# Four weight pieces on ScalarE's queue, and one 512 KB piece of V on the lower 64 partitions in 8-row transfers

## The chip, the cores and the metric

The kernel runs on one core of one Trainium2 chip. The time is the device time of one execution in microseconds (us), the median of several runs. Engines are written as in the profile: PE (TensorE matmul), PEld (its weight loads), DVE (VectorE), ACT (ScalarE), POOL (GpSimd), SP (SyncE, which issues most of the transfers). The core has 16 DMA engines, which move all transfers whatever engine issued them. A transfer adds 16 in all to its semaphore when it has landed.

## The reference, cut to what matters

Eight sequences (batches) of one token each pass twice through a layer of attention over a cache (A) and a mixing MLP (B). Both layers use the same caches and weights.

```python
B, Sq, D = 8, 1, 448
Hq, Hkv, Sk, Dh = 16, 8, 4096, 256

def _A_ref(x, k_cache, v_cache, wq, wo):
    q = (x @ wq).reshape(B, Sq, Hq, Dh).transpose(0, 2, 1, 3)
    k = jnp.repeat(k_cache, rep, axis=1)
    v = jnp.repeat(v_cache, rep, axis=1)
    p = _softmax(jnp.einsum("bhqd,bhkd->bhqk", q, k) * (Dh ** -0.5))
    o = jnp.einsum("bhqk,bhkd->bhqd", p, v)
    return o.transpose(0, 2, 1, 3).reshape(B, Sq, Hq * Dh) @ wo

x = x + _A_ref(_layernorm(x), k_cache, v_cache, wq, wo)
x = x + _B_ref(_layernorm(x), w1, w2, w3, w4)
x = x + _A_ref(_layernorm(x), k_cache, v_cache, wq, wo)
x = x + _B_ref(_layernorm(x), w1, w2, w3, w4)
```

With a sequence of one token the mixing of layer B adds nothing, so w1 and w2 aren't read: B is a norm, w3, gelu and w4. All numbers are bf16. One head of one batch has 4096 x 256 of K and as many of V, 2 MB each; there are 64 of each.

## The kernel before

**Tiles.** K and V live in a slab of 31 slots of 512 KB (128 partitions of 4 KB; `SLOT`, `NSLOT`, line 387). A head of K or V is four pieces ("chunks") of 512 KB, `c` = 0 to 3; partition p holds rows 32 p to 32 p + 31 of the cache, and piece c eight of these. Two heads `s` = 0, 1 are a pair, `m` = 0 to 3, of batch `b`. `chunks` (line 452) makes the load units of one head: `most` neighbouring pieces go in one transfer (512 KB, 1 MB or 2 MB), to as many neighbouring slots.

**Stages.** `kpart` computes the scores of a pair and their softmax: K is transposed on DVE (line 938) or on PE (line 856), multiplied with q on PE, and the exponentials P are written to `pT` (three buffers) with a transposed order of rows; some are also kept apart in `pN` (two buffers). `vpart` multiplies P with V on PE: with P as the moving side and V's 128x128 blocks as weights for the pairs called still (line 1089), with P as weights and V moving otherwise (line 1115); in the second form it then gathers the four partial sums (lines 1126 to 1141). `outproj8` applies wo (line 1178). `turn` is the MLP of one batch between its two attention layers, `end` the MLP of all batches at the very end. K of pairs 1 to 3 stays in its slots from the first layer to the second.

**Order.** Nothing of the order is written by hand: `Plan.schedule` simulates all engines with a cost for each operation and lays out the sequence of each engine's instructions. Among operations that are ready it takes the one with the smallest `prio`. Transfers go in the order of the list `order` (line 1278); each waits until its slots are free in that simulation, and each counts as 330 ns of SP. Groups of four or two can be split when no run of slots is free (lines 268 to 277). Every engine then runs its sequence in order, and waits on semaphores at what the plan found to be dependences.

**The start.** wq and w3 have 448 rows: three blocks of 128 and a rest of 64, which is folded into 128 partitions as two pieces of 64 partitions, `wqt0`, `wqt1` (256 KB each) and `w3t0`, `w3t1` (112 KB each). Piece 0 lies on partitions 0 to 63, piece 1 on 64 to 127. The pieces 1 (`U_side`) are issued from ACT's queue at the very start (line 1364); the pieces 0 (`U_even`) by SP, ahead of x (`U_s0`, 8 rows) and of the first K.

**The end.** In the last batch (b = 7) of the second layer, V comes in the order pair 1, 2, 3, 0 (lines 1267 and 1274), pair 3 in transfers of four pieces, pair 0 in transfers of two. Pair 0 is the last and is still: each piece is 16 matmuls of line 1089.

Of the kernel before, what the change touches and what calls it, by code (L numbers as in the profile page):

```python
# [3 lines left out]
P = 128  # L4
B = 8
# [6 lines left out]
NCH = 4  # L12
NSLOT = 31
SMALL = 220
SLOT = 2048
AHEAD = (1, 2)
NT = 2
NS = 2
NV = 2
# [54 lines left out]
class Unit:  # L74


    def __init__(self, name, emit, nbytes, slotted=True):
        self.name, self.emit, self.nbytes, self.slotted = name, emit, nbytes, slotted
        self.wide = None
        self.slot = self.sem = self.val = None  # L80
        self.op = None
        self.readers = []
        self.land = None
        self.evs = [None, None]
        self.raw, self.source = False, None
        self.side = False
        self.group, self.lead, self.pair = [self], None, None


class Plan:  # L90
# [79 lines left out]
    def schedule(self, order, nslot):  # L170
# [77 lines left out]
        while remaining or nxt[0] < len(order):  # L248
# [8 lines left out]
            while nxt[0] < len(order):  # L257
                u = order[nxt[0]]
                if any(d.end is None for d in u.op.deps):
                    break  # L260
                start = max(free["sp"], max((d.end + 80 for d in u.op.deps), default=0.0))
                us = u.group
                if u.slotted:
                    if len(us) == 1:
                        best = single(t)
                    else:
                        best, short = run(t, len(us))
                        if short and len(us) == 4 and transfer < t + DRY4:
# [12 lines left out]
                    start = max([start] + [slot_free[best + k][0] for k in range(len(us))])  # L281
                if start > t + 1e-6:
                    sp_next = start
                    break
                if u.slotted:
                    for k, x in enumerate(us):
                        _, waits = slot_free.pop(best + k)
                        x.slot = best + k
                        for w in waits:
                            u.op.deps[w] = True  # L290
                        live.append(x)
                        if x.raw:
                            raw.add(x)
                free["sp"] = start + 330.0
                if u.emit is not None:
                    transfer = max(start + 3300.0, transfer) + (P * 4096 * len(us) / 415.0 if len(us) > 1 else u.nbytes / 410.0)
                    land = transfer + 2000.0
                else:
                    land = start
                for x in us:  # L300
                    x.land = land
                u.op.on = "sp"
                seq["sp"].append(u.op)
                done(u.op, land, 0.0)
                nxt[0] += 1
                progress = True
# [54 lines left out]
def bass_interleave_layers__gqa_block_cached__mixer_s_mlp__decode_kernel(  # L361
# [33 lines left out]
    ident = sb("ident", [P, P], bf)  # L395
# [36 lines left out]
    def rows(u, t, ap, nbytes):  # L432
# [3 lines left out]
    U_wq = [rows(f"wq{k}", wq_sb[:, k, :], A_wq[k * P:(k + 1) * P, :], P * 8192) for k in range(3)]  # L436
    U_wq += [rows(f"wqt{i}", wqt_sb[64 * i:64 * i + 64, :], A_wq[3 * P:D, 2048 * i:2048 * i + 2048], 64 * 4096)
             for i in range(2)]
    U_side = [U_wq.pop()]
    U_w3 = [rows(f"w3{k}", w3_sb[:, k, :], B_w3[k * P:(k + 1) * P, :], P * 3584) for k in range(3)]  # L440
    U_w3 += [rows(f"w3t{i}", w3t_sb[64 * i:64 * i + 64, :], B_w3[3 * P:D, 896 * i:896 * i + 896], 64 * 1792)
             for i in range(2)]
    U_side.append(U_w3.pop())
    for u in U_side:
        u.side = True
    U_even = [U_wq.pop(), U_w3.pop()]
    wq_rest, w3_rest = ([U_side[i], U_even[i]] for i in range(2))
# [4 lines left out]
    def chunks(cache, b, h, name, skip=(), most=2):  # L452


        src = cache[b, h].rearrange("(p j) d -> p (j d)", p=P)

        def emit(e, u):
            c, n = int(u.name[-1]), len(u.group)
            return e.dma_start(slab[:, SLOT * u.slot:SLOT * (u.slot + n)], src[:, SLOT * c:SLOT * (c + n)])
        us = [None if c in skip else Unit(f"{name}{c}", emit, P * 4096) for c in range(NCH)]  # L460
        for i in range(0, NCH, most):
            group = [u for u in us[i:i + most] if u is not None]
            if len(group) == most:
                plan.load(group[0], mates=group[1:])
            else:
                for u in group:
                    plan.load(u)
        return us


    Bc = Buf()
# [388 lines left out]
    def kpart(at, layer, b, m, kept, most=2):  # L860
# [13 lines left out]
        p.x = x  # L874
        p.y = y = free_p.pop(0)
        p.z = z = free_n.pop(0) if layer == 0 and m > 1 else None
        plan.prio = at
        p.K, p.kload = [], []
        for s in range(2):
# [166 lines left out]
            430, [], [BpT[y]], [bS[x]], prio=pr, name=n + "pq")  # L1046
        for o in plain:
            plan.ops[-1].deps[o] = o.eng == "dve"
        for c in range(nn if z is None else 0):
            ss = slice(sum(c >= w for w in nns), 2)  # L1050
            add("act", lambda e, c=c, ss=ss: e.activation(apart(pT[y])[:, :, c, :, ss], xs.rearrange("p (a c r s) -> p a c r s", a=4, c=4, r=4)[:, :, c, :, ss],
# [6 lines left out]
    def vpart(at, p, still, bank, most, aside):  # L1058
# [5 lines left out]
        p.V = [u for s in range(2) for u in chunks(A_v_cache, b, 2 * m + s, f"{n}V{s}", (), most)]  # L1064
        p.vload = [u for u in p.V if u.lead is None]
        if layer == 0:
            out_, bo = o1[b % 2][:, 8 * m:8 * m + 8], Bo1[b % 2][m]
        else:
# [30 lines left out]
        else:  # L1099
# [3 lines left out]
            for s in range(2):  # L1103
                for c in range(NCH):
                    u = p.V[NCH * s + c]

                    def pv(e, u=u, c=c, s=s):
# [10 lines left out]
                    o = add("pe", pv, 430, Bp(s, c), [], [bV[x]], [u], prio=at + 0.02 * (NCH * s + c), name=f"{n}V{s}{c}", n=4)  # L1118
                    if s or c:
                        o.deps[first] = True  # L1120
                    else:
# [28 lines left out]
        if z is not None:  # L1150
            free_n.append(z)

    Bst = [{k: Buf() for k in ("pm", "gm", "mx")} for _ in range(NS)]

# [120 lines left out]
                weave(V(1, b, m, most=4 if m else 2))  # L1275
    plan.prio = 1e9
    U_out = end()
    order = U_side[:1] + U_even[:1] + U_side[1:] + U_even[1:] + [U_s0] + stream[:1] + U_wq + stream[1:10] + U_wo + stream[10:]
    order.append(U_s1)
    order.append(U_out)  # L1280
    seq = plan.schedule(order, NSLOT)
# [143 lines left out]
```

## Time and profile before

| what | value |
|---|---|
| runs | 1095.83, 1095.85, 1096.48 us; median 1095.85 |
| the profiled execution | 1096.3 us, of which the span of instructions is 1094.5 |
| busy, share of the span | PE 70%, PEld 48%, DVE 76%, ACT 19%, POOL 7% |
| transfers | 448.96 MB, mean 410 GB/s; 427 GB/s from 1036 to 1056 us |
| the chain that ended last | DVE 39%, DMA 26%, PE 20%, issue 7%, ACT 3% |
| granted PE clock, mean | 0.616 |
| SP's longest waits in total | for PE's V products of line 1115 294 us, for PE's scores of line 947 217 us |

A row of the stretches view has, after the stretch and its length, the busy time of PE, PEld, DVE, ACT and POOL with the number of their instructions, the granted PE clock, the DMA share (mean busy share of the 16 engines; packets that overlap on an engine can take it over 1) and GB/s. A row of the time order has start, duration, engine, line, operation, output and inputs, count, and in brackets the idle time before it and what ended it. A row of transfers has output and input, the issuing queue, count, KB of one and the median us from issue to landing.

The start, as the time order has it: ACT issues `wqt1` at 0.73 and `w3t1` at 1.32 us; SP issues `wqt0` at 0.74 (0.58 us), `w3t0` at 1.37 (0.83), x at 2.25 (0.53), the first K at 2.83 (0.37), then wq and more K. `ident`, which the first transposes need, is written by POOL at 9.94 us. The last three transfers of V are issued from 1051.88 to 1052.84 us.

### The profile page before, as it was taken

What the parts mean: (1) busy time and instruction counts of PE and PEld (TensorE: products, weight loads), DVE (VectorE), ACT (ScalarE), POOL (GpSimd) and SP (SyncE); (2) the same over time, 40 slices, a digit from 0 to 9 for tenths busy, and PEclk for the clock granted to TensorE, in tenths of its full rate; (3) what the DMA queues carried; (4) which work ended last, traced back from release to release, by engine and by line L of the source; (5) the groups of instructions that cost most, each with busy time, mean ns of one, the idle gap of its engine ahead of it and who ended that gap; (6) DMA issues with size and microseconds to landing.
All of it is one profiled execution on the core that took longest, in us unless ns stands there. A gap on an engine that the chain in (4) does not pass through costs nothing.

```text
span 1094.5 us, 33709 instructions
## 1 busy us (share of the span) xinstructions
PE 764.3 (70%) x15416; PEld 525.1 (48%) x15416; DVE 830.5 (76%) x1567; ACT 212.2 (19%) x322; POOL 72.0 (7%) x232
## 2 busy tenths in 40 slices
PE   3467586778677865778667786578766795676865
PEld 3255453465346543565336654365433654346533
DVE  5899549964997499954999569974799839996572
ACT  1023131113011311203202032121221231111310
POOL 0000000000000000000000010000100000000000
PEclk9998566556655665556655566555565666655655
DMA  9999999999999999999999999999999999999994
GB/s 357 405 420 417 411 400 428 422 404 409 428 422 417 411 428 426 422 395 423 426 426 419 399 423 426 426 416 398 427 428 424 400 406 426 426 423 414 416 425 188
DMA packets 54703, 448.96 MB, mean 410 GB/s; under 512 B 5520, under 2 KB 11552, under 8 KB 14112
## 3 DMA queue, kind: packets, MB, share of 16 engines
q1 hardware_dynamic: 54400, 446.42, 98.3%
q8 instruction: 121, 1.98, 0.7%
q10 hardware_dynamic: 160, 0.38, 0.1%
q14 instruction: 22, 0.18, 0.0%
HBM read 446.77 MB, written 0.01 MB: 408 GB/s over the span
## 4 chain that ended last, share of the span: by engine, by line
DVE 39%; DMA 26%; PE 20%; issue 7%; ACT 3%; POOL 1%; SPq 0%; DVEq 0%; POOLq 0%
DVE slots L938 31%; DMA slots<-in_A_k_cache_dram 17%; DMA slots<-in_A_v_cache_dram 9%; PE psV L1115 5%; PE psS L947 4%; DVE pT L1045 2%; PE psS L926 2%; PE psV L1089 2%; PE psT L609 1%; ACT slots L916 1%; DVE slots L1128 1%; PE psT L695 1%; PE psT L1163 1%; PE psK L856 1%; ACT slots L1217 1%
## 5 line engine op out<-in xcount | busy, mean ns | idle before, releaser
L938 DVE STREAM_TRANSPOSE slots<-slots 128x1024 bf16<-128x1024 bf16 x544 | 647.7, 1230 | 38.2 <-DMA slots<-in_A_k_cache_dram 25.1
L947 PE MATMUL psS<-qe,slots 128*128 128x8 bf16 x5760 | 225.4, 174 | 165.2 <-DVE slots L938 107.5
L947 PEld LDWEIGHTS psS<-qe,slots 128*128 128x128 bf16 x5760 | 190.5, 103 | 250.1 <-DVE slots L938 173.0
L1115 PE MATMUL psV<-slots,pT 128*8 128x512 bf16 x1528 | 183.7, 555 | 20.0 <-DMA slots<-in_A_v_cache_dram 15.2
L916 ACT COPY slots<-psK 128x1024 bf16<-128x1024 bf16 x80 | 78.6, 1015 | 165.1 <-PE psK L856 164.6
L856 PE MATMUL psK<-ident,slots 128*128 128x128 bf16 x640 | 75.1, 304 | 3.1 <-DMA slots<-in_A_k_cache_dram 2.9
L1009 POOL PARTITION_ALL_REDUCE small<-small x64 | 23.9, 374 | 720.4 <-DVE small L1007 586.0
L1126 ACT ACTIVATE slots<-psV 128x512 bf16<-128x512 f32 x48 | 28.8, 600 | 201.9 <-PE psV L1115 201.9
L856 PEld LDWEIGHTS psK<-ident,slots 128*128 128x128 bf16 x640 | 62.4, 141 | 5.7 <-DMA slots<-in_A_k_cache_dram 3.5
L975 PE MATMUL psS<-slots,qe 128*8 128x512 bf16 x200 | 55.3, 593 | 6.5 <-DVE slots L938 6.4
L1089 PE MATMUL psV<-pT,slots 128*128 128x2 bf16 x1568 | 50.6, 165 | 9.6 <-DMA slots<-in_A_v_cache_dram 9.0
L1115 PEld LDWEIGHTS psV<-slots,pT 128*8 128x8 bf16 x1528 | 31.5, 90 | 52.6 <-DMA slots<-in_A_v_cache_dram 21.5
L1089 PEld LDWEIGHTS psV<-pT,slots 128*128 128x128 bf16 x1568 | 47.2, 104 | 11.6 <-DMA slots<-in_A_v_cache_dram 9.1
L1128 DVE TENSOR_TENSOR slots<-psV,slots 128x512 bf16<-128x512 f32 x48 | 32.5, 677 | 25.2 <-ACT slots L1126 25.0
L1030 ACT ACTIVATE pT<-psS 128x128 bf16<-128x128 f32 x56 | 15.6, 279 | 173.6 <-DVE psS L1027 173.4
L1045 DVE STREAM_TRANSPOSE pT<-psS 128x128 bf16<-128x128 bf16 x64 | 45.2, 706 | 4.4 <-PE psS L1037 2.2
L1137 PE MATMUL psV<-same,slots 128*128 128x4 bf16 x320 | 14.2, 166 | 41.9 <-DVE slots L1128 36.8
L1163 PE MATMUL psT<-small,wo_sb 128*128 128x1 bf16 x1024 | 35.7, 166 | 7.1 <-DVE small L1096 4.7
L926 PE MATMUL psS<-qo,slots 128*128 128x2 bf16 x768 | 28.0, 167 | 13.4 <-ACT slots L916 10.4
L1163 PEld LDWEIGHTS psT<-small,wo_sb 128*128 128x128 bf16 x1024 | 32.5, 105 | 9.2 <-DVE small L1096 6.0
L1137 PEld LDWEIGHTS psV<-same,slots 128*128 128x128 bf16 x320 | 11.8, 103 | 49.6 <-issue 42.3
L1096 DVE TENSOR_TENSOR small<-psV,small 128x4 bf16<-128x4 f32 x30 | 4.3, 144 | 41.1 <-PE psV L1089 41.1
(178 smaller groups left out, 768.8 us busy)
## 6 DMA issues: line engine op xcount, KB each, us to landing
slots<-in_A_v_cache_dram SPq DMA_DIRECT2D x149, 1024.0 KB, 9.9
slots<-in_A_v_cache_dram SPq DMA_DIRECT2D x50, 2048.0 KB, 21.1
slots<-in_A_k_cache_dram SPq DMA_DIRECT2D x45, 2048.0 KB, 21.1
slots<-in_A_k_cache_dram SPq DMA_DIRECT2D x69, 1024.0 KB, 14.3
slots<-in_A_v_cache_dram SPq DMA_DIRECT2D x14, 512.0 KB, 8.0
wo_sb<-in_A_wo_dram SPq DMA_DIRECT2D x4, 896.0 KB, 19.1
wq_sb<-in_A_wq_dram SPq DMA_DIRECT2D x3, 1024.0 KB, 11.3
w_sb<-in_B_w_dram SPq DMA_DIRECT2D x1, 1568.0 KB, 15.2
```

Source lines behind the costliest of these rows:

```text
L856: last = e.transpose(tile[:, j * P:(j + 1) * P], slots[u.slot][:, o:o + P], ident[:, :])
L916: return e.copy(slots[u.slot][:, 1024 * t:1024 * t + 1024], tile)
L926: last = e.matmul(o, slots[u.slot][:, i:i + P], q, start=(cc == 0), stop=(cc == 1))
L938: return e.transpose(o, i)
L947: last = e.matmul(o, slots[u.slot][:, i:i + P], qe[:, 128 * k + 64 * s + 8 * g:128 * k + 64 * s + 8 * g + 8], start=(g == 0), stop=(g == 7))
L975: last = e.matmul(o, q, K[:, lo:hi + 1:hi - lo, :, g, :], start=(g == 0), stop=(g == 7))
L1045: add("dve", lambda e: e.transpose(pZ[:, :, 0:3:2].rearrange("p n s r -> p n r s"), psS[x][:, 128:192].bitcast(bf).rearrange("p (n r s) -> ...
L1089: last = e.matmul(o, slots[u.slot][:, i:i + P], w, start=(c == 0 and cc == 0 and j == 0), stop=(c == NCH - 1 and cc == 1 and j == 7))
L1115: last = e.matmul(psV[x][32 * i:32 * i + 8, :].rearrange("p (k d) -> p k d", k=2), w, v, start=(s == 0 and c == 0), stop=(s == 1 and c == ...
L1126: add("act", lambda e: e.activation(part(0), psV[x][:, :], ACT.Copy), 590, [], [Bhalf[0]], [bV[x]], [v], prio=at - 1, name=n + "ve0").targ ...
L1128: add("dve", lambda e: e.tensor_tensor(part(1), psV[x][:, :], part(0), ALU.subtract), 590, [Bhalf[0]], [Bhalf[1]], [bV[x]], [v], prio=at - ...
L1163: last = e.matmul(psT[:, 4 * (2 * s + i) + c:4 * (2 * s + i) + c + 1], wo_sb[:, a, d0:d0 + P], o1[b % 2][:, a:a + 1], start=(k == 0), stop ...
```

## The change

1. All four rest pieces go to ACT's queue, `wqt1`, `wqt0`, `w3t1`, `w3t0`; SP begins with x, then the first K.
2. In batch 7 of the second layer, pair 3, head 0, piece 3 of V (`LOW`): its upper 64 rows no longer go to the upper 64 partitions of a slot but to the lower 64 of a second slot. Each half is eight transfers of 8 rows; transfer i takes the rows r0, r0 + 4, ..., r0 + 28 with r0 = 32 (i // 4) + i % 4, to the partitions of the same numbers. The rest of that head goes as one pair of pieces and one single piece, where it could be one transfer of four.
3. P has to follow: a matmul with the right half of `ident` brings the upper 64 rows of P for that piece to the lower 64 partitions of PSUM, and ACT copies them to a `pN` buffer. The product of that piece is eight matmuls over 64 partitions instead of four over 128.
4. The last head of pair 0 (`B7m0V1`) is loaded in four single pieces instead of two pairs.
5. The plan counts 330 ns of SP for each of a unit's issues, and a slot's semaphore 16 for each.

```diff
+LOWS, LOWC = 0, 3
+def LOW(layer, b, m, s):
+    return (layer, b, m, s) == (1, B - 1, 3, LOWS)
...
-                free["sp"] = start + 330.0
+                free["sp"] = start + 330.0 * u.issues
...
-    U_side = [U_wq.pop()]
+    wq_rest = U_wq[3:]
+    del U_wq[3:]
...
-    U_side.append(U_w3.pop())
+    w3_rest = U_w3[3:]
+    del U_w3[3:]
+
+    U_side = wq_rest[::-1] + w3_rest[::-1]
     for u in U_side:
         u.side = True
-    U_even = [U_wq.pop(), U_w3.pop()]
-    wq_rest, w3_rest = ([U_side[i], U_even[i]] for i in range(2))
...
+        if low:
+            def half(p0):
+                def emit(e, u):
+                    for i in range(8):
+                        r0 = 32 * (i // 4) + i % 4
+                        d = e.dma_start(slots[u.slot][r0:r0 + 29:4, :], src[p0 + r0:p0 + r0 + 29:4, SLOT * LOWC:SLOT * (LOWC + 1)])
+                        if i < 7:
+                            d.then_inc(u.sem, 16)
+                    return d
+                return emit
+            most = 2
+            us[LOWC] = Unit(f"{name}{LOWC}", half(0), 64 * 4096)
+            us[LOWC].upper = Unit(f"{name}u{LOWC}", half(64), 64 * 4096)
+            us[LOWC].issues = us[LOWC].upper.issues = 8
         for i in range(0, NCH, most):
             group = [u for u in us[i:i + most] if u is not None]
-            if len(group) == most:
+            if len(group) == most and not name.startswith(f"B{B - 1}m0V1") and all(u.upper is None for u in group):
                 plan.load(group[0], mates=group[1:])
             else:
                 for u in group:
-                    plan.load(u)
+                    for w in (u, u.upper):
+                        if w is not None:
+                            plan.load(w)
...
+        if p.low:
+            low = psS[x][0:64, 192:208].rearrange("p (a r) -> p a r", a=4)
+            add("pe", lambda e: e.matmul(low, ident[:, 64:P], apart(pT[y])[:, :, p.place(LOWS, LOWC), :, LOWS], start=True, stop=True),
+                110, [BpT[y], Bc], [], [bS[x]], prio=pr, name=n + "lo", n=1)
+            add("act", lambda e: e.copy(apart(pN[zl])[0:64, :, 0, :, LOWS], low), 230, [], [BpN[zl]], [bS[x]], prio=pr, name=n + "lc")
...
+                    def low(e, u=u, c=c, s=s):
+                        for i in range(4):
+                            o, i_ = 12 * (NCH * i + p.place(s, c)) + 4 * s, 12 * i + 4 * s
+                            for w, v in ((pT[y][0:64, o:o + 8], u), (pN[p.zl][0:64, i_:i_ + 8], u.upper)):
+                                last = e.matmul(psV[x][32 * i:32 * i + 8, :].rearrange("p (k d) -> p k d", k=2), w,
+                                                slots[v.slot][0:64].rearrange("p (k j d) -> p j k d", k=2, j=4)[:, i], start=False, stop=False)
+                        return last
...
-    order = U_side[:1] + U_even[:1] + U_side[1:] + U_even[1:] + [U_s0] + stream[:1] + U_wq + stream[1:10] + U_wo + stream[10:]
+    order = [U_s0] + U_side + stream[:1] + U_wq + stream[1:10] + U_wo + stream[10:]
...
-            slot_n[u.slot] += 16
+            slot_n[u.slot] += 16 * u.issues
```

More of the change, by code (lines that the diff above doesn't have):

```diff
@@ L86, in __init__ @@
         self.side = False
+        self.upper = None
+        self.issues = 1
         self.group, self.lead, self.pair = [self], None, None
@@ L450, in bass_interleave_layers__gqa_block_cached__mixer_s_mlp__decode_kernel, with chunks @@
     U_w4 = [rows("w4", w4_sb[:, :, :], B_w4.rearrange("(t m) n -> m t n", m=P), P * 12544 * 1.1)]
-    def chunks(cache, b, h, name, skip=(), most=2):
+    def chunks(cache, b, h, name, skip=(), most=2, low=False):
         src = cache[b, h].rearrange("(p j) d -> p (j d)", p=P)
@@ L876, in kpart @@
         p.z = z = free_n.pop(0) if layer == 0 and m > 1 else None
+        p.low = LOW(layer, b, m, LOWS)
+        p.zl = zl = free_n.pop(0) if p.low else None
         plan.prio = at
@@ L1063, in vpart @@
         plan.prio = at
-        p.V = [u for s in range(2) for u in chunks(A_v_cache, b, 2 * m + s, f"{n}V{s}", (), most)]
-        p.vload = [u for u in p.V if u.lead is None]
+        p.V = [u for s in range(2) for u in chunks(A_v_cache, b, 2 * m + s, f"{n}V{s}", (), most, LOW(layer, b, m, s))]
+        p.vload = [w for u in p.V if u.lead is None for w in (u, u.upper) if w is not None]
         if layer == 0:
@@ L1117, in pv @@
                         return last
-                    o = add("pe", pv, 430, Bp(s, c), [], [bV[x]], [u], prio=at + 0.02 * (NCH * s + c), name=f"{n}V{s}{c}", n=4)
+                    def low(e, u=u, c=c, s=s):
[5 more added lines that the diff above has]
+                        return last
+                    if u.upper is not None:
+                        o = add("pe", low, 860, Bp(s, c) + [BpN[p.zl]], [], [bV[x]], [u, u.upper], prio=at + 0.02 * (NCH * s + c), name=f"{n}V{s}{c}", n=8)
+                    else:
+                        o = add("pe", pv, 430, Bp(s, c), [], [bV[x]], [u], prio=at + 0.02 * (NCH * s + c), name=f"{n}V{s}{c}", n=4)
                     if s or c:
@@ L1149, in vpart @@
         free_p.append(y)
-        if z is not None:
-            free_n.append(z)
+        for z_ in (z, p.zl):
+            if z_ is not None:
+                free_n.append(z_)
     Bst = [{k: Buf() for k in ("pm", "gm", "mx")} for _ in range(NS)]
```

## The prediction

> **What bounds the kernel.** I read the page first: the transfers.
>
> ```profile
> span 1094.5 us, 33709 instructions
> ...
> DMA  9999999999999999999999999999999999999994
> ...
> q1 hardware_dynamic: 54400, 446.42, 98.3%
> q8 instruction: 121, 1.98, 0.7%
> ```
>
> The sixteen DMA engines are busy in every slice but the last, so the time is the bytes over some 424 GB/s, plus a start, plus a tail behind the last landing. DVE (76%) and PE (70%) have room on average. The fetching of instructions (q8) costs 0.7% of 16 x 1094.5 us over 121 fetches: 1.0 us of one engine for each. So I looked where DMA is not full: the start, the end and the turns between batches. The stretches of the start:
>
> ```profile
> 2.00:3.00 1.00, 0.00 (x0) 0.00 (x0) 0.78 (x4) 1.00 (x1) 0.00 (x0) 1.00 0.71 188
> 3.00:4.00 1.00, 0.00 (x0) 0.00 (x0) 0.87 (x3) 0.25 (x1) 0.00 (x0) 1.00 1.04 274
> 4.00:5.00 1.00, 0.00 (x0) 0.00 (x0) 0.09 (x2) 0.00 (x0) 0.00 (x0) 1.00 1.01 215
> 5.00:6.00 1.00, 0.00 (x0) 0.00 (x0) 0.00 (x0) 0.00 (x0) 0.00 (x0) 1.00 1.32 264
> 6.00:7.00 1.00, 0.00 (x0) 0.00 (x0) 0.00 (x0) 0.00 (x0) 0.00 (x0) 1.00 0.73 262
> 7.00:8.00 1.00, 0.00 (x0) 0.00 (x0) 0.00 (x0) 0.00 (x0) 0.00 (x0) 1.00 0.98 410
> ```
>
> The last two columns are DMA share and GB/s. The engines are occupied from 3 us on, but move 215 to 274 GB/s, about half of the 424 seen later, while the four 64-partition pieces (wqt, w3t) are written: half of the partitions take half the rate. From 3 to 8 us 1.43 MB moved where 2.12 could have: 1.6 us lost. The end:
>
> ```profile
> 1076.00:1077.00 1.00, 0.71 (x27) 0.63 (x25) 0.19 (x1) 0.00 (x0) 0.00 (x0) 0.50 0.98 410
> 1077.00:1078.00 1.00, 1.00 (x41) 1.00 (x39) 0.24 (x1) 0.00 (x0) 0.00 (x0) 0.50 0.96 401
> 1078.00:1079.00 1.00, 0.73 (x28) 0.65 (x25) 0.48 (x3) 0.00 (x0) 0.00 (x0) 0.50 0.70 295
> 1079.00:1080.00 1.00, 0.48 (x16) 0.40 (x15) 0.19 (x1) 0.00 (x0) 0.00 (x0) 0.50 0.43 180
> 1080.00:1081.00 1.00, 0.95 (x32) 0.93 (x32) 0.00 (x0) 0.00 (x0) 0.00 (x0) 0.50 0.26 98
> 1081.00:1082.00 1.00, 0.06 (x3) 0.00 (x0) 0.00 (x0) 0.00 (x0) 0.00 (x0) 0.50 0.06 25
> ```
>
> The share runs out over four us: the engines don't finish together. The trace's completion counts (each engine adds one to a transfer's semaphore) give it singly for the last transfer: the first engine at 1078.18 us, the others 0.1, 0.1, 0.5, 0.7, 0.9, 1.3, 1.3, 1.8, 2.5, 2.7, 2.8, 2.8, 2.9, 3.1 and 4.3 us later. The last matmuls wait for that last one:
>
> ```profile
> 1080.05 1.01 PE L1089 MATMUL psV<-pT,slots 128*128 128x2 bf16 x32 [0.56 <-DMA slots<-in_A_v_cache_dram]
> 1082.51 1.01 PE L1089 MATMUL psV<-pT,slots 128*128 128x2 bf16 x32 [1.44 <-DMA slots<-in_A_v_cache_dram]
> 1083.55 0.18 DVE L1096 TENSOR_TENSOR qo<-psV,small 128x4 bf16<-128x4 f32 x1 [3.77 <-PE psV L1089]
> ```
>
> PE waits for the last megabyte until 1082.51, then needs 1.01 us for its 32 matmuls; the rest is a chain to 1094.5. Whatever brings the last landing forward shortens the kernel by as much.
>
> **Which engines are late.** Following the counts from transfer to transfer, each fetch of instructions puts one engine back by about 1.5 us, in turn over the same eight engines; the other eight are hit by the rare q14 fetches alone. The x transfer has 8 rows, and its count arrives as one jump and eight single steps: eight engines carry it. Six of these eight are among the late ones at the first K transfer, where five of the six late ones belong to those that fetches never hit. So I hold the eight engines of an 8-row transfer to be the unburdened ones; this is inferred, not shown.
>
> The Trainium skill ("DMA: Bandwidth & Descriptors", Why a DMA increments its semaphore by 16 and not by 1) says that the transfer runs on as many engines as divide its outer size, up to 16, and on this queue on the lowest-numbered ones. The x count of nine steps agrees with eight; which eight, no row shows.
>
> **Part 1, the start.** SP loses two issues (0.58 and 0.83 us) ahead of x and the first K; ScalarE's queue gains two of about 0.6 us, so its table load at 1.96 us ends 1.2 us later, 9 us before ACT's first work at 13.55. The DMA engines were already occupied without a gap from 2.07 us, so an earlier issue adds no bytes; the same pieces still go to the same halves at half rate, only with K between them. Nor does an earlier landing of x or K0 help: ident, which both wait for, comes from POOL at 10.2 us, and the norm's root waits for POOL until 19.86. Value 0; bounds -1.6 us (all of the lost rate comes back) and +0.3 (upper and lower pieces overlapped a little before, the row 274, and no longer do). A side effect: with x first, the list scheduler can put the root's DVE operations ahead of the first square (13.61, 1.23 us), which would then run after 21 us. DVE's next room covers that:
>
> ```profile
> 50.00:60.00 10.00, 3.90 (x68) 2.74 (x65) 6.46 (x7) 0.97 (x2) 0.37 (x1) 1.00 1.01 423
> ```
>
> 3.5 us of DVE are free there; without them it is +1.2.
>
> **Part 2, the pieces of the last batch.** One engine takes 159, 309 or 611 ns for a row of 4, 8 or 16 KB (medians of the packet records) and 9 ns for a completion. Head 0 of pair 3 was one transfer with 8 rows of 16 KB an engine: 4.89 us. Now a pair (8 x 0.309 = 2.47), a single (8 x 0.159 = 1.27), and sixteen 8-row transfers of one row an engine: 16 x 0.159 + 15 x 0.009 = 2.68 on eight engines, nothing on the other eight. The eight take 6.42 (+1.5), the others 3.74 (-1.15). The last head of pair 0 in four singles instead of two pairs: 32 x 0.159 + 4 x 0.009 against 16 x 0.309 + 2 x 0.009, +0.16 for all. Together +1.7 and -1.0. If the burdened eight are the eight latest, the last of them ends at 4.3 - 1.0 = 3.3 and the last of the others at 1.3 + 1.7 = 3.0: -1.0. If the one at 1.8 or 2.5 is of the others (a q14 fetch hit one at 1002 us), that one ends at 3.5 to 4.2: -0.8 to -0.1. I take -0.6; bounds -1.0 and +1.7 (the last engine itself is one of the eight that take more).
>
> **Part 3, the tail.** The last landing holds one piece instead of two; the piece before it lands some 1.2 us earlier and is done meanwhile. 16 matmuls instead of 32: -0.5. Bounds -0.5 and 0.
>
> **Part 4, costs I put at nothing.** SP: 17 more issues for pair 3 and 2 for pair 0, 19 x 0.377 us (median of the nine there) = 7.2 us, 10.1 at the x issue's 0.53. Behind them wait pair 3's second head and all of pair 0. Cover: in this stretch transfers land long after issue,
>
> ```profile
> slots<-in_A_v_cache_dram SPq DMA_DIRECT2D x5, 2048.0 KB, 19.9
> slots<-in_A_v_cache_dram SPq DMA_DIRECT2D x4, 1024.0 KB, 26.7
> ```
>
> for 5 and 2.5 us of moving, so over 14 us of queue stand ahead. Without that cover, +7 to +10. PE: four matmuls more (four took 0.39 us at 1066.5) and one of 16 columns, in a stretch where it waits 3.6 us for DMA; ACT's copy of 0.3 us falls in an idle time of 3.2 us; the slot more is taken when K slots have been given back (last K scores at 1061). Their P is ready 10 us before use. If the cover went, 0.3 to 0.7 us.
>
> **Sum.** 0 - 0.6 - 0.5 = -1.1 us on the profiled execution, 1096.3 us (1094.5 of span and 1.8 around it), which lies 0.45 over the median 1095.85: the median becomes 1094.8.
>
> **Rivals.**
> A, the start pays: K between the half pieces lets their writes catch up and 1.6 us comes back, which the unbroken DMA carries to the end; with half of the spread of part 2: 1095.85 - 1.1 - 1.6 - 0.2 = 1092.9. For: 215 GB/s is waste. Against: the bytes per half are unchanged.
> B, small transfers pay a fixed price on the eight engines, at pair 3's last piece. From 3.0 + 16p > 3.3, p = 0.02 us, they end last; at p = 0.11 the gain is gone; at 0.25 it is 0.2% slower. Nearest row: the 1.6 us lost between 3 and 8 us over five small transfers, 0.32 each: 16 x 0.32 = 5.1, the end at 8.1 instead of 4.3, less 0.5: +3.3, 1099.2. Against: the stretch 1036 to 1056 has a share of 100% with transfers back to back. The Trainium skill ("DMA: Bandwidth & Descriptors", Rules for kernel authors) says that transfers under 64 KB are mostly overhead and should be joined; by its 0.68 us for 4 KB the sixteen would be an estimated 11 us. The start's rows lie below that.
> C, the plan is made anew: the earlier x shifts choices of the list scheduler, and other slots come free late at the turns, where the queue nearly drains (361 GB/s at 140 to 150 us). One square (1.23 us) late in four of eight turns: +4.9 - 1.1, 1099.7. Against: the transfers' order and lengths are the same until the last batch.
> D, the 8 rows use all engines, or the wrong eight: only the tail is left, 1095.4.
>
> **How the numbers follow.** Forecast 0.50, A 0.17, B 0.15, C 0.13, D 0.05. Its own range is 1093.4 to 1096.1. The joint one, 1092.5 to 1098.6, takes in most of A, D, and B and C where they are mild. 0.2% (2.2 us) is about what a measurement here tells from no change: faster A and an edge of the forecast, 0.22; slower most of B and C, 0.26; same 0.52.
>
> **What would show it.** Right: the DMA share at the end falls within some three us instead of four, the last PE group has 16 matmuls, the start still shows 215 to 270 GB/s and wq lands as before. Wrong: over 400 GB/s by 5 us (A); the end held up by eight engines alone, a share of 0.5 for long (B); other turns, lower GB/s there (C).

## The result and the profile after

| | before | after |
|---|---|---|
| runs, one next to the other | 1094.05 to 1098.37 us, median 1095.61 (13) | 1095.63 to 1100.08 us, median 1097.36 (13) |
| the profiled execution | 1096.3 us, span 1094.5 | 1099.78 us, span 1098.0 |
| the last landing of V | 1082.46 us | 1086.41 us |
| from there to the end of the span | 12.04 us | 11.59 us |

The ratio is 1.0021, with a 95% interval of 1.0012 to 1.0030: the change makes the kernel slower, by 1.3 to 3.3 us. The profiled execution of after is 2.4 us over its own median, so its span of 1098.0 isn't to be set against 1094.5 as a whole; what follows compares stretches. The page of after:

```profile
DMA  9999999999999999999999999999999999999994
...
q1 hardware_dynamic: 54928, 446.04, 98.2%
```

As before, DMA is full in all slices but the last. The packets of q1 (SP's queue) are 528 more: the smaller pieces of V add more than the two rest pieces take away that went to ACT's queue. The fetches of instructions are 121, as before. The stretches of the start of after (DMA share and GB/s last):

```profile
5.00:6.00 1.00, 0.00 (x0) 0.00 (x0) 0.00 (x0) 0.00 (x0) 0.00 (x0) 1.00 1.02 422
6.00:7.00 1.00, 0.00 (x0) 0.00 (x0) 0.00 (x0) 0.00 (x0) 0.00 (x0) 1.00 1.14 303
7.00:8.00 1.00, 0.00 (x0) 0.00 (x0) 0.00 (x0) 0.00 (x0) 0.00 (x0) 1.00 0.96 233
8.00:9.00 1.00, 0.00 (x0) 0.00 (x0) 0.00 (x0) 0.00 (x0) 0.00 (x0) 1.00 0.97 276
9.00:10.00 1.00, 0.00 (x0) 0.00 (x0) 0.00 (x0) 0.00 (x0) 0.00 (x0) 1.00 1.05 369
10.00:11.00 1.00, 0.00 (x0) 0.00 (x0) 0.00 (x0) 0.00 (x0) 0.00 (x0) 1.00 1.00 342
11.00:12.00 1.00, 0.03 (x1) 0.04 (x2) 0.06 (x1) 0.00 (x0) 0.28 (x1) 1.00 1.04 337
12.00:13.00 1.00, 0.23 (x4) 0.14 (x4) 0.73 (x10) 0.00 (x0) 0.00 (x0) 1.00 0.98 332
```

The slow stretch that ended at 7 us before now lasts to 13 us, at a full DMA share. Before, the stretches from 7 to 13 us moved 410 to 442 GB/s. K comes through from 5 to 6 us, but the rest pieces then trickle: the completion counts show `wqt0` landed at 9.86, `w3t1` at 12.10 and `w3t0` at 13.82 us, where before all four had landed by 6.72. The packet records show the delay in the rows of K and wq too: one of 8 KB takes a median of 473 ns from 6 to 9 us and 378 ns from 9 to 13 us, and 309 ns in before from 100 us to 1000 us. Adding the GB/s column from 2 to 13 us gives 3.73 MB before and 3.40 MB after: 0.33 MB less, or 0.8 us at 424 GB/s. The end of after, in stretches:

```profile
1081.00:1082.00 1.00, 1.00 (x41) 1.00 (x39) 0.36 (x1) 0.00 (x0) 0.00 (x0) 0.50 0.86 340
1082.00:1083.00 1.00, 0.77 (x29) 0.69 (x27) 0.37 (x2) 0.00 (x0) 0.00 (x0) 0.50 0.52 213
1083.00:1084.00 1.00, 0.78 (x29) 0.70 (x27) 0.16 (x1) 0.00 (x0) 0.00 (x0) 0.50 0.19 78
1084.00:1085.00 1.00, 0.54 (x16) 0.46 (x16) 0.04 (x1) 0.00 (x0) 0.00 (x0) 0.50 0.17 70
1085.00:1086.00 1.00, 0.58 (x16) 0.50 (x16) 0.00 (x0) 0.00 (x0) 0.00 (x0) 0.50 0.08 29
1086.00:1087.00 1.00, 0.54 (x16) 0.50 (x16) 0.00 (x0) 0.00 (x0) 0.00 (x0) 0.50 0.06 16
```

and PE in order of time:

```profile
1083.96 0.58 PE L1123 MATMUL psV<-pT,slots 128*128 128x2 bf16 x16 [0.22 <-DMA slots<-in_A_v_cache_dram]
1085.20 0.58 PE L1123 MATMUL psV<-pT,slots 128*128 128x2 bf16 x16 [0.66 <-DMA slots<-in_A_v_cache_dram]
1086.46 0.58 PE L1123 MATMUL psV<-pT,slots 128*128 128x2 bf16 x16 [0.67 <-DMA slots<-in_A_v_cache_dram]
```

From 1083 us on the share is 0.19 and less: some three of sixteen engines still work, and then one, and PE takes one piece of 16 matmuls after the other as these engines bring them. The counts of the last transfer lie 0, 0.7, 1.5, 1.5, 1.6, 2.1, 2.2, 2.2, 2.5, 2.5, 2.7, 2.9, 3.0, 4.5, 4.9 and 5.8 us after the first: a spread of 5.8 us, where before it was 4.3. What follows the last landing is 0.45 us shorter.

### The profile page after: what moved, and what is told of

Read it like the earlier page. It is cut to its first block, busy times and chain, and to the rows that moved or that the text cites. A ratio compares the mean times of both kernels' runs of the same rounds, so it can differ in the third digit from the quotient of the medians.

```text
span 1098.0 us, 33739 instructions
## 1 busy us (share of the span) xinstructions
PE 762.1 (69%) x15421; PEld 523.7 (48%) x15421; DVE 830.8 (76%) x1567; ACT 212.4 (19%) x323; POOL 71.6 (7%) x232
## 4 chain that ended last, share of the span: by engine, by line
DVE 36%; DMA 27%; PE 21%; issue 8%; SPq 4%; ACT 4%; POOL 1%; DVEq 0%; POOLq 0%
DVE slots L966 27%; DMA slots<-in_A_k_cache_dram 15%; DMA slots<-in_A_v_cache_dram 12%; PE psV L1149 6%; PE psS L975 5%; SPq L440 3%; DVE pT L1073 2%; PE psS L954 2%; PE psV L1123 2%; DVE slots L1173 1%; PE psT L635 1%; ACT slots L944 1%; SPq L469 1%; PE psK L882 1%; ACT slots L1263 1%
```

## The experiments

Three numbers are read from each profile besides the time. **L12**: the mean landing (over the sixteen counts) of the thirteenth transfer to the slots, a transfer of K issued at 45.4 to 47.4 us, which shows how far the start is behind; the expectations call it the thirteenth K transfer. **Spread**: from the first to the last count of the last transfer of V. **To end**: from the mean landing of the last transfer of pair 1 of batch 7 to the end of the span (which is read to 0.1 us); it leaves out all that happened before. Diffs are against the changed kernel where nothing else is said. "The start of before" is

```diff
-    wq_rest = U_wq[3:]
-    del U_wq[3:]
+    U_side = [U_wq.pop()]
...
+    U_even = [U_wq.pop(), U_w3.pop()]
+    wq_rest, w3_rest = ([U_side[i], U_even[i]] for i in range(2))
...
-    order = [U_s0] + U_side + stream[:1] + U_wq + stream[1:10] + U_wo + stream[10:]
+    order = U_side[:1] + U_even[:1] + U_side[1:] + U_even[1:] + [U_s0] + stream[:1] + U_wq + stream[1:10] + U_wo + stream[10:]
```

and "the end of before" is

```diff
-    return (layer, b, m, s) == (1, B - 1, 3, LOWS)
+    return False
...
-            if len(group) == most and not name.startswith(f"B{B - 1}m0V1") and all(u.upper is None for u in group):
+            if len(group) == most and all(u.upper is None for u in group):
```

All in one table; the text on each follows. The ratios are to runs of the kernel before made next to them (medians 1095.38 to 1095.78 us); they aren't the quotient of two medians, and where the two columns differ the text goes by the ratio and its interval.

| kernel | median, us | ratio, 95% interval | MB, 2 to 13 us | L12, us | spread, us | to end, us |
|---|---|---|---|---|---|---|
| before | | 1 | 3.73 | 56.26 | 4.28 | 44.27 |
| after | 1097.36 | 1.0021 [1.0012, 1.0030] | 3.40 | 57.08 | 5.77 | 44.80 |
| start_only | 1098.13 | 1.0013 [1.0002, 1.0024] | 3.25 | 57.63 | 4.13 | 44.06 |
| start_plan | 1094.76 | 0.9999 [0.9986, 1.0011] | 3.78 | 56.16 | 3.43 | 43.35 |
| start_pairs | 1097.02 | 1.0008 [0.9997, 1.0018] | 3.72 | 56.32 | 3.10 | 43.30 |
| start_sp | 1096.50 | 1.0002 [0.9992, 1.0012] | 3.77 | 56.60 | 4.22 | 44.27 |
| start_mix | 1095.86 | 1.0003 [0.9993, 1.0014] | 3.68 | 56.39 | 2.94 | 43.29 |
| low_only | 1096.99 | 1.0004 [0.9993, 1.0015] | | 55.90 | 5.87 | 44.97 |
| end_only | 1095.58 | 0.9997 [0.9987, 1.0007] | | 56.39 | 6.14 | 44.68 |
| low_twice | 1097.44 | 1.0021 [1.0011, 1.0031] | | 56.38 | 5.59 | 45.72 |
| low_16 | 1098.25 | 1.0017 [1.0008, 1.0027] | | 56.17 | 4.09 | 46.94 |
| singles_only | 1095.00 | 0.9997 [0.9985, 1.0008] | | 56.08 | 4.13 | 44.04 |
| end_plain | 1095.69 | 0.9993 [0.9983, 1.0004] | | 56.21 | 4.00 | 43.59 |
| probe | 1094.14, one run | | | 56.33 | 3.40 | 43.54 |

**The parts alone.** start_only has the end of before, so of the change it keeps the four pieces on ACT's queue and x first.

> Only the start of the change: all four rest pieces on ScalarE's queue, SP begins with x and K; the last batch as before. Theory S (mixing half-partition pieces with K costs DMA time): the K transfers issued in the first 7 us land on the mean of the sixteen engines 0.8 us later than before (first engine +1.0, last engine about 0), from 20 to 120 us, and the kernel takes 0 to +0.8 us. Rival (the start is free, as predicted): mean within 0.2 us, time 0. Rival C (a new plan): other jumps at the turns, present in every run.

The start alone is slower by 0.13% (0.2 to 2.6 us), and L12 is 1.4 us late, more than the 0.8 of after and the 0.8 that was expected. The trace has the same slow stretches, 221 to 344 GB/s from 6 to 13 us. The end is that of before in every number.

low_only has the start of before and pair 0 in pairs; only the piece in 8-row transfers is left:

```diff
-            if len(group) == most and not name.startswith(f"B{B - 1}m0V1") and all(u.upper is None for u in group):
+            if len(group) == most and all(u.upper is None for u in group):
```

> Only the piece in 8-row transfers; the start and the last head of pair 0 (two pairs) as before. Theory L (some of the eight engines that carry the 8-row transfers are among the late ones): the last transfer's sixteen counts spread over 5.5 to 6 us instead of 4.3, its last count is 1.2 to 2.0 us further behind pair 2's last transfer than before, and the kernel takes +1.0 to +2.0 us. As predicted (the eight are the unburdened ones): spread about 3.3, time -0.6. Rival B (a fixed price p for each small transfer): the eight engines are behind by 1.5 + 16 p, all of them alike, so that the last counts of the piece come at more than 0.25 us from one another on each engine.

The spread is 5.9 us, and "to end" is 1.2 us over the mean of the seven kernels that end as before (43.29 to 44.27, mean 43.73), and 0.7 us over before alone. The time, 1.0004, doesn't show it: its interval (0.8 us faster to 1.6 slower) holds both nothing and 1.2 us.

singles_only has the start of before and `LOW` returns False; the last head in four single pieces is left.

> Only the last head of pair 0 in four single pieces; start and pair 3 as before. Theory: 0.16 us more of transfers for rows of 4 KB, and 16 matmuls instead of 32 behind the last landing, -0.45 us from the last landing to the end: 12.04 becomes 11.6; the kernel takes -0.3 us. Rival (the four issues or the smaller rows cost as much as the tail gives): 0.

The part behind the last landing is 11.66 us, 0.4 less than the 11.92 to 12.09 of the kernels with pairs. The time is that of before within its interval. end_plain is the same, and takes the change's division of pair 3's head 0 (a pair and two single pieces) too, but in ordinary transfers over 128 partitions:

```diff
+        if name.startswith(f"B{B - 1}m3V0"):
+            most = 2
...
-            if len(group) == most and not name.startswith(f"B{B - 1}m0V1") and all(u.upper is None for u in group):
+            if len(group) == most and not (name.startswith(f"B{B - 1}m0V1") or name.startswith(f"B{B - 1}m3V0") and i == 2) and all(u.upper is None for u in group):
```

> Pair 3's head 0 as a pair and two single pieces, piece 3 in one ordinary transfer over 128 partitions, the last head of pair 0 in four singles; the start as before. What is left of the end of the change when no small transfers and no uneven load are in it. Theory L: no cost but smaller rows, +0.3 us of transfers, -0.45 of tail: -0.1 us, the last spread 4.3 as before. Rival (the splitting itself, with its issues and slots, is what costs): +1 us or more here too.

Its spread is 4.0 us, so the division of the head doesn't widen it; the 8-row form does. It has the lowest ratio of all, 0.9993, but the interval reaches over 1, so it can't be called faster than before.

**What of the start costs.** start_plan keeps the changed order of all instructions, the DVE operations of the norm's root ahead of the squares included, and issues the transfers as before. The end of before is in all four of these.

```diff
         if e == "act":
-            for u in U_side:
+            for u in U_side[0::2]:
                 u.emit(eng, u).then_inc(u.sem, 16)
+        if e == "sp":
+            for u in U_side[1::2]:
+                u.emit(eng, u).then_inc(u.sem, 16)
```

> The instruction order of the changed kernel at the start (the two squares of DVE behind the root), but the four rest pieces are issued as before: uppers from ACT, lowers by SP ahead of x and K. The end is that of before. Theory S (the time goes where half-partition pieces share the engines with whole transfers): the mean landing of the thirteenth K transfer is at 56.3 us as before, the time within 0.1% of before. Rival D (the squares' late place costs): the landings at 57 us or later, and the time of start_only, +0.13%.

L12 is at 56.16, the ratio 0.9999 (1.5 us faster to 1.2 slower): the order of DVE costs nothing up to L12 and nothing that the time shows, as theory S has it. start_pairs puts x first on SP, then the lower pieces on SP beside the upper ones on ACT (`U_side[0::2]` alone is issued from ACT and marked as side).

> x goes first on SP, and then the rest pieces lower and upper side by side from SP and ACT again, all ahead of the first K. The end is that of before. Theory S: like before, the thirteenth K lands at 56.3 us in the mean, time within 0.1%. Rival X (it is the early x that costs): 57.1 to 57.6 us and +0.13%. If only the last lower piece still overlaps K, between the two, some +0.3 us.

The landings are those of before (56.32), so the early x costs nothing up to there either. The time, 1.0008, lies between the two expectations, and its interval (0.3 us faster to 2.0 slower) holds both.

start_sp asks whether it is the sharing with K and wq that costs, or that an upper and a lower piece are no longer written side by side: all four go from SP.

```diff
-        if e == "act":
+        if e == "sp":
             for u in U_side:
                 u.emit(eng, u).then_inc(u.sem, 16)
```

> All four rest pieces in the changed kernel's order (upper, lower, upper, lower), but all from SP, ahead of x and of the first K; nothing of them from ACT. The end is that of before. So no piece shares the engines with a whole transfer of the other queue, and no upper piece is written beside its lower one. Theory S (the sharing with whole transfers costs): the mean landing of the thirteenth K transfer at 56.0 to 56.6 us, time within 0.1% of before. Theory P (what is lost is the writing side by side of an upper and a lower piece): 57.0 us or later, +0.1%.

56.60 us, at the edge of what S gave, 3.77 MB by 13 us, ratio 1.0002: writing side by side isn't needed. start_mix takes the last step: the pieces stand behind x and K's first transfer, as in the change, but in SP's one queue.

```diff
-        if e == "act":
-            for u in U_side:
-                u.emit(eng, u).then_inc(u.sem, 16)
...
                     o.unit.emit(eng, o.unit).then_inc(o.unit.sem, 16)
+                    if o.unit is stream[0]:
+                        for u in U_side:
+                            u.emit(eng, u).then_inc(u.sem, 16)
```

> As start_sp, but SP issues x and the first K transfer ahead of the four rest pieces, which stand between that K transfer and wq in the one queue. The end is that of before. Theory Q (what costs is that two queues share each engine row by row while half pieces are written, and in one queue transfers follow one another): the thirteenth K lands at 56.0 to 56.6 us in the mean, the stretches from 8 us on show 400 GB/s and more, time within 0.1% of before. Rival K (half pieces behind any whole transfer cost): 57.0 us or later, some 340 GB/s until 13 us, +0.1%.

The stretches of start_mix:

```profile
6.00:7.00 1.00, 0.00 (x0) 0.00 (x0) 0.00 (x0) 0.00 (x0) 0.00 (x0) 1.00 0.99 256
7.00:8.00 1.00, 0.00 (x0) 0.00 (x0) 0.00 (x0) 0.00 (x0) 0.00 (x0) 1.00 1.06 254
8.00:9.00 1.00, 0.00 (x0) 0.00 (x0) 0.00 (x0) 0.00 (x0) 0.00 (x0) 1.00 1.18 310
9.00:10.00 1.00, 0.00 (x0) 0.00 (x0) 0.00 (x0) 0.00 (x0) 0.00 (x0) 1.00 0.92 360
10.00:11.00 1.00, 0.00 (x0) 0.00 (x0) 0.00 (x0) 0.00 (x0) 0.00 (x0) 1.00 1.00 418
```

K's first transfer lands at 6.93 us, earlier than the 8.08 of the change; then come four slow stretches, and from 10 us on 418 and more. (The expectation put the return to 400 at 8 us; the slow part only stands two us later.) L12 is at 56.39, ratio 1.0003. So at the start half pieces cost their four or so slow microseconds wherever they stand in one queue. When they share the engines with whole transfers from another queue, the slow part lasts to 13 us, and L12 is 0.8 and 1.4 us later (57.08 and 57.63, against 55.90 to 56.60 in the twelve other kernels). The times of start_mix and start_only don't tell the two apart: their intervals overlap.

**Which eight engines.** probe is the kernel before with four tiny transfers behind the last V, and a small DVE instruction for each at the end:

```diff
+    U_seen = [Unit(f"seen{i}", lambda e, u, i=i, n=n: e.dma_start(seen[0:n, 4 * i:4 * i + 4], A_x[0:n, 0, 4 * i:4 * i + 4]), 8 * n, slotted=False)
+              for i, n in enumerate((1, 2, 4, 8))]
```

> The kernel before with four more transfers behind the last V, of 1, 2, 4 and 8 rows with 8 bytes a row, to read which engines they wait for; and one small DVE instruction for each at the end. If the eight engines of an 8-row transfer were those that fetches don't hit, its eight counts would arrive within 1.5 us of each other, and well after the first landing. If they are a mix, as the counts of the changed kernel let expect, they spread over 2.5 us or more, with some among the first and some among the last of the sixteen.

The completion counts, in us:

```
last V   1076.98 1077.13 .25 .28 .51 .60 1078.00 .30 .48 .85 1079.09 .23 .26 .48 1080.16 .38
1 row    1077.15
2 rows   1077.33 1078.65
4 rows   1077.46 .50 .69 1078.82
8 rows   1077.31 .63 .68 .80 .86 1078.99 1079.68 1080.57
```

The eight counts span 3.3 us. A count comes 0.17 to 0.20 us after the one before it on the same engine, which tells whose it is: five of the engines are among the first six to finish V, one is in the middle, one late, and one the very last. The counts of the sixteen small transfers in after say the same: the eight that carry them stood at 0, 0.06, 0.36, 0.39, 0.39, 2.4, 2.7 and 3.6 us in the transfer ahead of the piece (0 is its first count), the last of them the latest of all sixteen. The eight are a mix, and the latest engine is among them.

**More of it, and the same bytes on all engines.** low_twice gives pair 2 the same piece as pair 3 (start of before, end of the change):

```diff
-    return (layer, b, m, s) == (1, B - 1, 3, LOWS)
+    return (layer, b, s) == (1, B - 1, LOWS) and m in (2, 3)
```

> The start of before; V's piece 3 of head 0 goes to the lower partitions in 8-row transfers for pair 3 as in the change and for pair 2 too; the last head in single pieces. Theory L (eight engines carry all of each such piece, and no fetch evens that out): the last transfer's counts spread over 7.4 us or more (5.9 with one piece, 4.3 before), and from the last transfer of pair 1 to the end it takes 1.4 us more than before, twice the 0.7 of low_only; time +0.1 to +0.2%. Rival F (a fixed price of small transfers on all engines): the spread stays at 5.9 and the mean landing is later by as much as the last. Rival N (the spread in low_only was chance): 4 to 6 us again, and the time of before.

The time is 0.21% over before (1.2 to 3.4 us), "to end" 2.0 us over the mean of 43.73 where one piece gave 0.9 to 1.2. But the spread stays at 5.6, and the mean landing of the last transfer, counted from that of pair 1, is 30.74 us where it was 29.94 with one piece and the same end (end_only). Neither theory has both. SP in order of time shows why:

```profile
1039.19 10.84 SPq L474 DMA_DIRECT2D slots<-in_A_v_cache_dram  x16
1050.13 1.33 SPq L467 DMA_DIRECT2D slots<-in_A_v_cache_dram  x3
1051.50 10.65 SPq L474 DMA_DIRECT2D slots<-in_A_v_cache_dram  x16
1062.19 1.93 SPq L467 DMA_DIRECT2D slots<-in_A_v_cache_dram  x4
```

Each run of 16 issues holds SP for over 10 us, 0.67 us for one. Pair 3's second head is issued at 1062.19, when the first of the engines that carry nothing of the pieces had finished all it had: the counts of the transfer ahead of the second set begin at 1061.86. The two first of these (1061.86 and 1062.78) would have landed its 4.9 us of moving by 1066.8 and 1067.7; they land at 1069.42 and 1069.50, together with two others. These two ran dry until SP's issue reached them, and lost 2.6 and 1.8 us. That is 0.3 of the 0.8 us in the mean, and it keeps the spread down by as much as the first was held up (5.6 instead of 8.2). Two late engines took both pieces and are last again (5.5 and 5.6 us, the next one 3.7), as theory L has it. The rest of the 0.8 isn't accounted for; 0.35 of it falls on the first single piece of pair 0, late on all engines but the last two.

low_16 has the start and last head of before, and moves the piece in eight transfers of 16 rows:

```diff
-                    for i in range(8):
-                        r0 = 32 * (i // 4) + i % 4
-                        d = e.dma_start(slots[u.slot][r0:r0 + 29:4, :], src[p0 + r0:p0 + r0 + 29:4, SLOT * LOWC:SLOT * (LOWC + 1)])
-                        if i < 7:
+                    for i in range(4):
+                        r0 = i
+                        d = e.dma_start(slots[u.slot][r0:r0 + 61:4, :], src[p0 + r0:p0 + r0 + 61:4, SLOT * LOWC:SLOT * (LOWC + 1)])
+                        if i < 3:
```

> The start and the last head of before; the one piece of V goes to the lower partitions in transfers of 16 rows, eight in all, so that the same bytes go to the same half but all sixteen engines carry them. Theory L (the imbalance of eight engines costs): the last transfer's counts spread over 3.1 to 4.3 us as in the kernels without the piece, and the time is that of before within 0.1%. Rival H (the half of the partitions costs): the piece takes twice its time, 1.2 us more, in the mean landing of the last transfer, and +0.1%. Rival F (the small transfer costs): more than 1 us in the mean as well, but with the engines apart as before.

The stretches in which low_16 writes the piece:

```profile
1060.00:1062.00 2.00, 1.91 (x50) 1.15 (x48) 1.09 (x4) 0.26 (x1) 0.37 (x1) 0.94 1.11 313
1062.00:1064.00 2.00, 1.38 (x21) 0.56 (x21) 0.70 (x2) 0.77 (x3) 0.43 (x2) 1.00 0.97 281
1064.00:1066.00 2.00, 0.61 (x8) 0.11 (x8) 1.00 (x3) 0.52 (x1) 0.09 (x1) 1.00 1.14 311
1066.00:1068.00 2.00, 0.39 (x4) 0.09 (x4) 0.00 (x0) 0.00 (x0) 0.00 (x0) 0.76 1.03 254
```

and the same place in low_only, with eight rows:

```profile
1062.00:1064.00 2.00, 1.52 (x38) 0.76 (x35) 0.76 (x4) 0.67 (x1) 0.37 (x1) 0.96 1.04 424
1064.00:1066.00 2.00, 1.81 (x29) 0.67 (x29) 1.03 (x3) 0.78 (x3) 0.52 (x2) 1.00 1.11 453
1066.00:1068.00 2.00, 0.39 (x4) 0.09 (x4) 0.69 (x1) 0.10 (x1) 0.00 (x0) 1.00 1.01 426
```

Rival H holds, and more strongly than it was priced: the spread is that of the plain kernels (4.1), but the rate falls to 254 to 313 GB/s, the mean landing is 3.0 us late (32.67 us after pair 1's, 29.68 before), and the time is 0.17% up. The packets say the same: from 1064 to 1068 us a row of 4 KB takes a median of 283 ns and one of 16 KB 1046 ns in low_16, and 159 and 613 ns in low_only. The 8-row form loses no rate: its piece costs 1.29 us in the mean landing (6.19 us to the next 2 MB, which alone take 4.90), like 512 KB in one ordinary transfer (1.27).

The loss in low_16 is over twice the 1.2 us that the bytes per half would give, and in one queue. Ahead of the piece its engines stood 3.6 us apart (in start_mix 1.3 us at the first K), so some wrote half rows while others wrote whole rows. That is what the two queues bring about at the start; that it is the same loss isn't tested.

end_only puts the end of the change behind the start of before.

> The start of before, the whole end of the changed kernel. If the parts add up: spread of the last transfer 5.5 to 6 us, 11.6 us from there to the end, from the last transfer of pair 1 to the end 44.4 to 44.9 us against 43.3 to 44.3 in the kernels without the piece, time 0 to +0.1%. If the change's +0.21% comes from the end after all: +0.15% or more.

The stretch values are as expected: spread 6.1, 11.60 us from there to the end, "to end" 44.68. The time, 0.9997, lies just under the range given, and its interval (1.4 us faster to 0.8 slower) ends just short of the 0.9 us that "to end" is over 43.73. So the time doesn't confirm a cost of the end.

## Why the prediction was wrong

The forecast was 1.1 us faster; measured is 1.3 to 3.3 us slower. 1097.4 us lies within the joint range, and above the likeliest case's own (1093.4 to 1096.1).

**Part 1, the start: value 0, at worst +0.3. This step failed.** Measured is 0.8 us at L12 in the profile of after, 1.4 us in that of start_only, and +0.13% (0.2 to 2.6 us) in the time of start_only. The sentence that carried it, "the same pieces still go to the same halves at half rate, only with K between them", took the loss to be fixed by the bytes per half. In one queue at the start this is so (start_sp, start_mix); beside whole rows from a second queue it isn't, and the whole rows take longer (473 and 378 ns instead of 309 for 8 KB). Rival A saw K between the pieces as a possible gain, and no case had it as a loss. The views show that the slow part lasts longer, and the experiments that at the start two queues are needed for it; why half rows of one queue hold up whole rows of another so much isn't shown.

**Part 1, the rest: right.** The root's operations went ahead of the square, as foreseen; in after the first squares run here, after the root:

```profile
20.04 3.49 DVE L966 STREAM_TRANSPOSE slots<-slots 128x1024 bf16<-128x1024 bf16 x3
```

In before one square ran at 13.61 and two more at 19.94 and 22.35 us, and the fourth began at 23.82; in after all three follow the root, which began 1.3 us earlier (18.53), and the fourth begins at 23.76. So DVE had caught up by 24 us, and the room after 50 us wasn't needed. start_plan has the same order (fourth square at 23.90), and its time shows no cost.

**Part 2, the pieces: -0.6, with bounds of -1.0 and +1.7. Wrong in sign, inside the bounds.** The step that failed is "I hold the eight engines of an 8-row transfer to be the unburdened ones". Six of eight late at the first K transfer is little evidence, and late there needn't be late at the end; the probe shows a mix with the latest engine in it. The price of the rows was right: 1.29 us in the mean of sixteen engines is 2.58 us on eight, where 2.68 was put. The case named as upper bound, "the last engine itself is one of the eight that take more", is what happened: the spread is 5.6 to 6.1 us in four kernels with 8-row pieces and 2.9 to 4.3 (mean 3.7) in nine that move no half piece at the end. The engines that carry nothing of the piece finish earlier, which widens the spread at no cost, so not all of this 2 us is lost: "to end" is 0.9 to 1.2 us over 43.73 in the three kernels with one piece. The Trainium skill ("DMA: Bandwidth & Descriptors", Why a DMA increments its semaphore by 16 and not by 1) puts a transfer that uses k engines on the k lowest-numbered ones on this queue; the steps of 1, 2, 4 and 8 counts in the probe agree in number, and no row here gives the engines' numbers.

**Part 3, the tail: -0.5. Right**: 12.04 to 11.59 us, and 11.58 to 11.66 in each kernel with single pieces at the end. No time shows it by itself (singles_only 0.9997, 1.6 us faster to 0.9 slower).

**Part 4, the costs at nothing: right for this change, with a price that was too low.** An issue took 0.72 us in the mean, not 0.38 or 0.53:

```profile
1046.90 11.49 SPq L476 DMA_DIRECT2D slots<-in_A_v_cache_dram  x16
1058.43 5.76 SPq L469 DMA_DIRECT2D slots<-in_A_v_cache_dram  x4
```

11.5 us for the 16. The 14 us of queue ahead covered them: the head issued at 1058.43 lands from 1070.62 on, 12.2 us later, while the DMA share stays at 0.97 and more. low_twice has the same end with that cover gone, and there two engines lose 2.6 and 1.8 us to SP.

**The rivals.** B, a fixed price on the eight engines: the sixteen rows took 2.58 us where 2.68 was put, so p is nothing. (The counts of a late engine come 0.18 to 0.21 us apart during the piece; they fall behind, and the transfer that follows makes it up.) The rule of the Trainium skill ("DMA: Bandwidth & Descriptors", Rules for kernel authors) on transfers under 64 KB doesn't show in these rows on the engines' side: by its 0.68 us the sixteen would have taken 11 us, and 2.58 us were measured. What was dear is the issue: SP took 0.72 us for 32 KB, and 0.33 to 0.44 for 2 MB. C, another plan: on each engine the traces show the same order until the last batch, but for DVE's at the start and a few neighbours that change places later (DVE at 100.6 and 159 us, PE at 175 us), and start_plan, which has this plan, isn't slower; C isn't borne out. D: the wrong eight engines was true, but it isn't neutral, as D had it.

**What stays open.** The parts alone give +1.4 us (start_only, 0.2 to 2.6) and -0.3 us (end_only, -1.4 to +0.8), together 1.1; the whole gives 2.3 (1.3 to 3.3). The intervals overlap. That the start costs something is shown by time, from 0.2 us up; that the end costs something is shown by the profiles' stretches, and by a time only for two pieces, whose issues also held up SP (low_twice).

Of the 3.5 us between the two profiled spans, 0.8 lie before L12 and 0.5 behind the last transfer of pair 1. The other 2.2 lie between the two, where the transfers are the same; the fourteen profiles take 992.4 to 996.1 us there (before 994.0, after 996.1). The six kernels with the changed order of DVE take 995.3 us in the mean and the eight others 993.7, so the profiles don't exclude that this order costs something far behind the start. The time of start_plan leaves room for 1.2 us at most.

## What to carry to other kernels

Transfers that fill half of the partitions from all sixteen engines lost more than their bytes when whole rows moved beside them, here from a second queue; at the start, in one queue, they didn't. Look at GB/s against the DMA share, since the share stays at 1 while the rate halves. A transfer that uses fewer than all engines moves the balance between them, and what it adds is still there at the last landing, so it needs to be known which engines are late before such a one is placed; four tiny transfers at the end and their completion counts show it for that execution. Issues that cost nothing behind a full queue can cost time at the second use, when the cover has been spent.

## What the hardware showed that was not expected

512 KB to half of the partitions cost 1.29 us in the mean landing when eight engines wrote them and the other eight went on with whole rows (424 to 453 GB/s), and some 2.9 us more when all sixteen wrote them (254 to 313 GB/s). SP's issue of an 8-row transfer of 32 KB took 0.67 to 0.72 us in a run of sixteen, while its issue of 2 MB took 0.33 to 0.44.
